# The cosine as one Sin with its turns on ScalarE and VectorE, and a new order for the feed-forward's list

## The chip, the cores and the metric

The kernel runs on one core of one Trainium2 chip. The metric is the device time of one execution in microseconds (us), taken as the median of three runs. Engines are named as in the profile: PE is TensorE's matmuls and PEld its weight loads, DVE is VectorE, ACT is ScalarE, POOL is GpSimd, and SP is SyncE, whose queue issues all DMAs of the feed-forward.

## The reference, cut to what is computed

An attention with a window of 32 tokens and 32 global tokens (4 batches, 8 heads, 512 + 32 tokens, 64 wide) gives x of 2176 tokens by 512. Two feed-forward layers of width 2048 follow:

```python
def _moe_ref(x, w_in, w_out):
    h = x @ w_in
    sp = np.where(h > 20.0, h, np.log1p(np.exp(np.minimum(h, 20.0))))
    g = h * np.tanh(sp)
    return (g @ w_out).astype(np.float32)

def _moe2_ref(x, w_in, w_out):
    h = x @ w_in
    g = h * np.cos(h)
    return (g @ w_out).astype(np.float32)
```

The weight matrices arrive as 64-bit floats, 512 by 2048 and 2048 by 512 for each layer, so the kernel itself has to make 32-bit values of them.

## The kernel before

The attention comes first, by a list of its own (`ORDER`), which the change leaves alone. Beside the attention the first weights are converted and the first products of layer 0 are made. After it, `feed_forward` runs the string `ORDER2`: a list, written out in full, of some 2,700 short steps such as `M0:25` or `h0:24d`. Each step issues one or a few instructions on one engine, in the order of the list; an engine executes its own instructions strictly in that order, and semaphores make it wait for what other engines or DMAs must have done. A letter at the end of a step picks the engine where there is a choice: `a` is ScalarE, `d` VectorE. Where a step stands in the list relative to the steps of another engine binds nothing by itself.

**The work of PE.** The tokens form duos of 768, 768 and 640 columns, the hidden width of a layer 8 pairs of 256. A step number s (0 to 41) is one duo and one pair: steps 0 to 17 are layer 0 (duos of 768, 768 and 640 with six pairs each; the other pairs of layer 0 are worked off ahead, in steps `u` and `lp`), 18 to 41 layer 1 with eight pairs a duo. The pairs of the second duo are taken in reverse. Every value is split into a high and a low part, and a product is the sum of three matmuls. `M0` to `M6` (`product`, L928) are the seven products that give the two halves of the hidden block, by a scheme with sums of blocks that saves one product in eight; each is 6 matmuls of 384 or 320 columns. They go through two PSUM banks: M0, M2, M3 and M4 through bank 0, M1, M5 and M6 through bank 1. `r0`, `r1`, `r2` (`keep`) copy bank 0 out after M0, M2 and M3, and `H00`, `H01`, `H11`, `H10` (`plus` and a copy) give the four quarters of the hidden block after M1, M4, M5 and M6. The next product into the same bank waits for that copy. `U0` to `U11` (`unit`, L1007 in layer 0 and L1011 in layer 1) multiply the activated block by the output weights into six more banks: 8 units a step in layer 0, 12 or 10 in layer 1. The units of step s run among the products of step s+1.

**The activation.** In layer 0 `A` and `B` are Mish on ACT. In layer 1 `gates` makes h cos h for each half c of a step: `k` adds a large constant to h/2pi on ACT (`nearest`, L957), `K` takes it away again on ACT, in a few steps on DVE (`nearest2`, L963, L961), `t` is h/2pi less that on DVE (`turns`, L966), `i` is Sin of pi times it on ACT (L969), `j` its square times 2 on ACT (L972), `p` is (1 - that) times h on DVE (`times`, L975). `h` then splits off the high part on ACT or DVE (L289, L287), and `l` makes the low part on DVE (L809). All work in place on the tile `ks`, one of 768 columns for each half. The last step, 41, does this in quarters of 320 columns.

**The weights.** A piece n (0 to 91) is a quarter or so of a pair's weights. Layer 0's pairs 2 to 7 are pieces 8 to 43, layer 1's pairs 8 to 15 are 44 to 91, six to a pair; piece 89 is the sum block that product M2 of pair 15 reads. `cc` loads the raw words (three buffers `raw`), `cr` is the rounding word (ACT or DVE), `cp` and `cq` the sign (ACT or DVE), `cb` a shift, `cs` the join, `ct` the sign's product, `cx0` to `cx3` the sums of blocks (all DVE), `ch` the high part (ACT or DVE), `cl` the low part (DVE), and `cw` writes the finished piece to DRAM (`scr`). Pieces 8 to 43 are made in the very tiles from which PE reads them. Pieces 44 to 91 go through two staging tiles `co`, taken in turns: `ch` of piece n waits until the DMA of `cw` of piece n-2 has landed. `W0` to `W5` (`fetch`, L914) bring a pair's weights back from `scr` into the tiles `weights` and `even`: W0 for M0 and M1, W1 for M3 and M6, W2 for M4 and M5, W3 for M2, W4 and W5 for the units. A fetch waits on SP's queue for the landing of the `cw` whose bytes it reads and for the last product that read its tile; whatever stands behind it on that queue waits too. Layer 1's first duo (steps 18 to 25) takes the pairs 8 to 15 for the first time, the other duos fetch them again.

Of the kernel before, what the change touches and what calls it, by code (L numbers as in the profile page):

```python
# [75 lines left out]
    u:22 cx3:9 v:9a cb:12 ch:10a st:4 cs:12 u:23 cc:15 v:10a ct:12 cr:14a v:11d pa:0 cl:10 st:5 pa:1 lp:2 pl:0 ch:9a
    cw:10 pl:1 cp:14a cl:9 cq:14a lp:3 T3:0 cw:9 pw:2 cb:13 cs:13 u:24 cc:18 pw:3 ct:13 I4:0a u:25 I3:0d cr:15a L4:0
    u:26 cp:15a L3:0 cq:15a u:27 pa:2 pa:3 lp:4 pl:2 pl:3 lp:5 pw:4 ch:11d cl:11 cw:11 u:28 pw:5 u:29 v:12a u:30 v:13a
    st:6 u:31 v:14a v:15d pa:4 pa:5 lp:6 pl:4 st:7 pl:5 lp:7 pw:6 u:32 pw:7 I5:0d I6:0a L5:0 u:33 T0:1 u:34 u:35 L6:0
    u:36 T1:1 pa:6 pa:7 u:37 pl:6 v:16a pl:7 u:38 v:17a st:8 u:39 v:18a M0:0 v:19a st:9 M1:0 r0:0a u:40 H00:0 u:41 u:42  # L80
# [1028 lines left out]
```

## Time and profile before

| | |
|---|---|
| median of 3 runs | 857.52 us (856.78 to 858.04) |
| profiled execution, its own time | 855.49 us |
| span of its trace | 853.6 us |
| busy share of the span, PE / PEld / DVE / ACT / POOL | 98% / 89% / 75% / 69% / 10% |
| mean granted clock of TensorE, share of full speed | 0.998 |

The span runs from the first to the last instruction; the execution's own time is 1.89 us longer. The feed-forward's products of step 0 start at 213.0 us into the span, the last matmul starts at 849.3 us. A busy share is the union of an engine's instructions over the span. Durations of single matmuls overlap, so the pace of PE is read from the distance between groups.

### The profile page before, as it was taken

The numbers are of one execution on the slowest core, as the hardware profiler recorded it, in microseconds if no ns is written. First come the engines' busy times: TensorE is split into PE (matmuls) and PEld (weight loads), VectorE is DVE, ScalarE is ACT, GpSimd is POOL, SyncE is SP. The second block draws the span as 40 slices with busy tenths as digits, with TensorE's granted clock in tenths as the row PEclk, the third lists the DMA queues.
The fourth block names the chain that finished last, engine by engine and source line by source line (L and its number), as shares of the span: only waits on it lengthen the run. The fifth ranks groups of instructions, "written<-read, shape, count | busy, mean of one in ns | idle before, by whom it ended". The sixth has DMA issues, their size and how long they took to land.

```text
span 853.6 us, 16057 instructions
## 1 busy us (share of the span) xinstructions
PE 839.9 (98%) x5883; PEld 761.0 (89%) x5883; DVE 638.1 (75%) x1336; ACT 590.7 (69%) x1151; POOL 82.1 (10%) x138
## 2 busy tenths in 40 slices
PE   8999999999999999999999999998999999999998
PEld 6788888999999989999999989887889989899996
DVE  6887675794699988759876999999766556865654
ACT  6998888784689967456554587887665455765565
POOL 4664555000000000000000000000000000000000
PEclk9999999999999999999999999999999999999999
DMA  8976852342799899997899889988466556376741
GB/s 179 213 155 163 202 133 64 112 174 83 234 344 319 295 318 350 386 317 237 318 378 354 309 305 337 327 311 292 139 213 198 179 184 184 100 243 224 224 145 66
DMA packets 141565, 198.69 MB, mean 233 GB/s; under 512 B 78896, under 2 KB 98352, under 8 KB 141488
## 3 DMA queue, kind: packets, MB, share of 16 engines
q1 hardware_dynamic: 141488, 197.67, 72.1%
q8 instruction: 47, 0.77, 0.4%
q14 instruction: 30, 0.25, 0.1%
HBM read 148.36 MB, written 49.28 MB: 232 GB/s over the span
## 4 chain that ended last, share of the span: by engine, by line
PE 90%; DMA 3%; ACT 3%; DVE 2%; issue 1%; POOL 0%; SPq 0%; DVEq 0%; POOLq 0%; ACTq 0%
PE bank L928 32%; PE acc L1011 20%; PE acc L1007 15%; PE acc L835 5%; PE h L452 4%; PE s L585 2%; DMA scr<-co 2%; PE av L656 2%; PE bank L452 2%; PE ta L629 2%; PE av L650 1%; PE avg L733 1%; DMA raw<-in_moe_w_in_dram 1%; PE qt L547 1%; PE sg L673 1%; PE kt L561 1%
## 5 line engine op out<-in xcount | busy, mean ns | idle before, releaser
L1011 PE MATMUL acc<-weights,g 128*128 128x512 f32 x816 | 202.7, 394 | 0.3 <-DVE g L809 0.2
L1011 PEld LDWEIGHTS acc<-weights,g 128*128 128x128 f32 x816 | 152.1, 189 | 28.4 <-DVE g L809 0.5
L1007 PE MATMUL acc<-g,weights 128*128 128x512 f32 (+1 forms) x864 | 154.0, 327 | 0.0
L1007 PEld LDWEIGHTS acc<-g,weights 128*128 128x128 f32 x864 | 134.1, 188 | 9.9
L289 ACT COPY r<-bank 128x384 f32<-128x384 f32 (+1 forms) x96 | 44.4, 463 | 113.9 <-PE bank L928 113.5
L943 DVE TENSOR_TENSOR hs<-r,bank 128x384 f32<-128x384 f32 (+1 forms) x126 | 66.8, 530 | 68.7 <-PE bank L928 60.0
L928 PE MATMUL bank<-xo,weights 128*128 128x384 f32 (+1 forms) x504 | 92.7, 328 | 3.9 <-DMA weights<-scr 3.8
L928 PEld LDWEIGHTS bank<-xo,weights 128*128 128x128 f32 x504 | 83.5, 189 | 6.4 <-ACT ks L972 4.1
L966 DVE SCALAR_TENSOR_TENSOR ks<-hs,ks 128x768 f32<-128x768 f32 (+2 forms) x50 | 44.0, 880 | 36.9 <-ACT ks L963 36.7
L605 ACT ACTIVATE pr<-pr,nm 128x160 f32<-128x160 f32 x128 | 53.6, 425 | 6.1 <-DVE nm L602 5.6
L969 ACT ACTIVATE ks<-ks 128x768 f32<-128x768 f32 (+2 forms) x50 | 39.3, 786 | 18.3 <-DVE ks L966 18.2
L289 ACT COPY hs<-bank 128x384 f32<-128x384 f32 (+1 forms) x41 | 18.9, 461 | 47.0 <-PE bank L928 46.9
L835 PE MATMUL acc<-g,weights 128*128 128x384 f32 (+1 forms) x288 | 48.9, 326 | 0.3 <-DVE xT L780 0.3
L928 PE MATMUL bank<-xs,weights 128*128 128x384 f32 (+1 forms) x252 | 48.4, 326 | 0.7 <-ACT r L289 0.7
L928 PE MATMUL bank<-xl,weights 128*128 128x384 f32 (+1 forms) x252 | 48.7, 328 | 0.0
L928 PE MATMUL bank<-xl,even 128*128 128x384 f32 (+1 forms) x252 | 48.6, 328 | 0.0
L928 PE MATMUL bank<-xs,even 128*128 128x384 f32 (+1 forms) x252 | 48.3, 326 | 0.0
L835 PEld LDWEIGHTS acc<-g,weights 128*128 128x128 f32 x288 | 47.6, 188 | 0.4 <-DVE xT L780 0.4
L402 DVE CUSTOM_DVE_ANT_0 bits<-bits,round 128x1024 uint16<-128x1024 uint16 x64 | 45.6, 713 | 1.3
L975 DVE SCALAR_TENSOR_TENSOR ks<-ks,hs 128x768 f32<-128x768 f32 (+2 forms) x50 | 43.9, 878 | 3.5 <-ACT ks L972 2.6
L384 ACT ACTIVATE round<-raw,magic 128x512 f32<-128x512 uint32 x49 | 37.1, 760 | 13.5 <-DVE bits L402 6.7
L809 DVE TENSOR_TENSOR g<-ks,g 128x768 fp32r<-128x768 f32 (+2 forms) x50 | 44.2, 883 | 2.8 <-ACT g L289 1.3
(175 smaller groups left out, 1618.8 us busy)
## 6 DMA issues: line engine op xcount, KB each, us to landing
weights<-scr SPq DMA_DIRECT2D x112, 512.0 KB, 4.7
even<-scr SPq DMA_DIRECT2D x48, 512.0 KB, 4.8
scr<-co SPq DMA_DIRECT2D x40, 512.0 KB, 5.8
raw<-in_moe_w_out_dram SPq DMA_DIRECT2D x28, 512.0 KB, 6.6
raw<-in_moe_w_in_dram SPq DMA_DIRECT2D x26, 512.0 KB, 6.4
scr<-weights SPq DMA_DIRECT2D x21, 512.0 KB, 5.3
weights<-scr SPq DMA_DIRECT2D x32, 256.0 KB, 5.1
scr<-even SPq DMA_DIRECT2D x9, 512.0 KB, 4.4
```

The lines of the kernel that those rows point to most:

```text
L289: nc.scalar.copy(out=out, in_=in_)
L402: nc.vector.tensor_tensor(out=bits(n), in0=bits(n), in1=tiles["round"][:, piece[n] % 2].bitcast(I32), op=ALU.add)
L452: nc.tensor.matmul(t[:, 0:m], l[:, k], r, start=k == 0 and i == 0, stop=k == NK - 1 and i == 2)
L605: nc.scalar.activation(out=pr[:, i], in_=pr[:, i], func=AF.Exp, bias=nm[:, i:i + 1], scale=-1.0, accum_out=l[:, i:i + 1])
L809: nc.vector.tensor_tensor(out=out, in0=x, in1=y, op=ALU.subtract)
L835: nc.tensor.matmul(o, l[:, a * P:(a + 1) * P], r[:, c], start=g == 0 and c == 0 and k == 0, stop=g == 1 and c == 1 and k == 2)
L928: nc.tensor.matmul(to, w[:, l, i + c], x[r][:, c], start=o in (0, 1, 5) and c == 0 and m == 0, stop=c == 1 and m == 2, skip_group_check=True)
L943: nc.vector.tensor_tensor(out=h_of(s, c, i), in0=tiles["r"][:, r, 0:n], in1=tiles["bank"][1][:, 0:n], op=ALU.add)
L966: nc.vector.scalar_tensor_tensor(out=k(s), in0=h(s), scalar=INV2PI, in1=k(s), op0=ALU.mult, op1=ALU.subtract)
L975: nc.vector.scalar_tensor_tensor(out=k(s), in0=k(s), scalar=1.0, in1=h(s), op0=ALU.subtract, op1=ALU.mult, reverse0=True)
L1007: nc.tensor.matmul(o, l[:, cols], r[:, part], start=start and m == 0 and i * a % 2 == 0, stop=stop and m == 2, skip_group_check=True)
L1011: nc.tensor.matmul(tiles["acc"][a], l[:, cols], r, start=start and m == 0, stop=stop and m == 2)
```

## The change

The cosine is computed another way. `k` (`shift`) now makes h/2pi + 0.25 on ACT; `K` (`nearest`) adds and subtracts the large constant in one instruction on DVE and writes the nearest whole number to a new tile `wide`; `t` subtracts it from `ks` on DVE; `i` is one Sin of 2 pi times that on ACT; `j` is gone; `p` is a plain product with h on DVE. The functions can put some of these on GpSimd by a letter `g`, which the new list doesn't contain.

The list `ORDER2` is new from end to end. It holds the same steps but for the 50 `j`. What moved, counted over the list: K in 48 places from ACT to DVE (all 50 are now on DVE); 12 of the steps cp, cq and cr, 17 of r0, r1 and r2 together, 7 of h, 4 of I (the high parts of the inputs) and 2 of ch from DVE to ACT; smaller exchanges elsewhere. The order of PE's products and units is changed inside each step, with the same instructions in number and shape: in layer 0 from `M0 M1 U0 U1 U2 M2 U3 U4 U5 M3 M5 M4 U6 M6 U7` to `M0 U0 M1 U1 M2 U2 U3 M5 M3 U4 M4 U5 M6 U6 U7`, in layer 1 as the two stretches of step 36 in the diff show. The pieces' steps stand earlier or later: the `cw` of piece 89, say, stands after `M0:24` where it stood before `M6:24`.

The diff, cut to its core (the stretches of the list that are shown are around `M0:1`, `M0:6`, `M0:24` and `M0:36`):

```diff
...
-    r2:0a ct:14 cr:18a M4:0 cb:15 ch:14a H11:0 cc:20 u:46 cs:15 cp:18a cl:14 H01:0a M6:0 A0:0 ct:15 cw:14 u:47 H10:0
-    B0:0 cx0:15 y1:0 M0:1 v:22a cx2:15 l0:0 v:23a M1:1 A1:0 st:11 cx1:15 U0:0 cb:18 ch:17a cx3:15 r0:1a cc:21 cl:17 U1:0
...
-    M1:6 ct:43 r0:6a T3:1 I5:1a U0:5 W0:8 H00:6 ch:43a U1:5 L5:1 B1:5 U2:5 cl:43 I4:1a l1:5 cw:43 cc:44 I6:1a M2:6 L4:1
-    U3:5 r1:6a W3:8 L3:1 U4:5 L6:1 U5:5 e0:0 M3:6 T0:2 cc:45 f0:0 cr:44a M5:6 e1:0 y3:0 r2:6a f1:0 cp:44a T1:2 M4:6 y0:1
...
-    U11:22 k1:23 cs:87 M0:24 p0:23 K1:23a M1:24 ct:87 r0:24a W0:25 h0:23a cx0:87 M2:24 W0:27 t1:23 cq:90a W3:27 l0:23
-    W5:24 r1:24a i1:23 cx1:87 U0:23 H00:24 j1:23 U1:23 cx2:87 ch:87d M3:24 cp:91a cl:87 cq:91a p1:23 U2:23 cw:87 r2:24a
-    M5:24 cr:91a cx3:87 h1:23d ch:88a M4:24 l1:23 U3:23 H11:24 H01:24a W2:27 cl:88 U4:23 k0:24 cs:90 W1:25 U5:23 cw:88
-    ch:89a K0:24d U6:23 cl:89 U7:23 t0:24 cw:89 M6:24 ct:90 i0:24 U8:23 cb:91 W1:27 j0:24 H10:24 U9:23 T0:4 U10:23 k1:24
-    U11:23 p0:24 K1:24a W2:25 M0:25 h0:24d W3:25 ch:90a l0:24 M1:25 r0:25a I0:4a t1:24 I1:4a H00:25 cl:90 i1:24 L0:4
-    cw:90 j1:24 M2:25 T1:4 U0:24 r1:25a p1:24 U1:24 T2:4 M3:25 h1:24a W4:25 cs:91 I2:4a U2:24 l1:24 M5:25 r2:25a I3:4a
...
-    h0:35d M0:36 l0:35 W5:36 M1:36 t1:35 r0:36a M2:36 H00:36 W0:38 i1:35 U0:35 j1:35 r1:36d W3:38 U1:35 p1:35 M3:36
-    h1:35d M5:36 l1:35 r2:36a M4:36 H11:36 U2:35 H01:36a W2:38 U3:35 k0:36 U4:35 K0:36a U5:35 W4:37 t0:36 U6:35 M6:36
-    i0:36 U7:35 j0:36 H10:36 W1:38 U8:35 k1:36 p0:36 U9:35 K1:36a h0:36d M0:37 l0:36 W5:37 M1:37 t1:36 r0:37a M2:37
...
+    ct:15 B0:0 u:46 H10:0 ch:14a u:47 l0:0d v:22a v:21a cl:14d v:23a st:10 cx0:15d M0:1 cw:14 A1:0 st:11 cx2:15d cx3:15d
+    ch:17a U0:0 cx1:15d r0:1a cl:17d ch:16a cb:18 M1:1 cw:17 cs:18d ch:15a y1:0 U1:0 B1:0 cl:16d H00:1 cw:16 cp:18a M2:1
...
+    cl:37d U6:3 ch:38a cb:39 W1:7 cw:37 H10:4 B0:4 U7:3 cl:38d cr:39a l0:4d cw:38 M0:5 cq:39a cc:44 cs:39d A1:4 U0:4
...
+    U1:5 W0:8 I4:1a H00:6 M2:6 cp:44a cl:43d cr:44a U2:5 T3:1d cw:43 W3:8 r1:6a L4:1d U3:5 cq:44a I6:1a cb:44 M5:6
...
+    cq:90a cl:86d r2:23a ct:87 U2:22 cw:86 cr:91a H11:23 U3:22 cp:91a cx0:87d M4:23 cx1:87d cq:91a ch:87d cl:87d M6:23
+    H01:23a cx2:87d k0:23 cw:87 U4:22 cx3:87d W0:25 H10:23 ch:88a U5:22 K0:23d k1:23 U6:22 W4:24 t0:23d U7:22 K1:23d
+    i0:23 U8:22 t1:23d U9:22 W1:25 ch:89a p0:23d U10:22 i1:23 U11:22 cl:89d h0:23a cl:88d M0:24 cw:89 W5:24 l0:23d cw:88
+    M1:24 r0:24a p1:23d M2:24 W0:27 H00:24 h1:23a cb:90 U0:23 W3:25 W3:27 r1:24a cs:90d U1:23 l1:23d M3:24 ct:90 M5:24
+    r2:24a cb:91 W2:25 cs:91d ch:90a U2:23 H11:24 U3:23 cl:90d M4:24 ct:91 cw:90 M6:24 T0:4d ch:91a W2:27 H01:24a cl:91d
+    U4:23 W1:27 k0:24 H10:24 U5:23 cw:91 T1:4d k1:24 U6:23 U7:23 K0:24d W4:25 t0:24d U8:23 U9:23 K1:24d i0:24 U10:23
+    t1:24d U11:23 p0:24d i1:24 M0:25 h0:24d M1:25 l0:24d W5:25 r0:25a I0:4a M2:25 p1:24d I1:4a H00:25 U0:24 r1:25a L0:4d
...
+    M0:36 W5:36 p1:35d M1:36 r0:36a h1:35d M2:36 W0:38 H00:36 l1:35d U0:35 r1:36a W3:38 U1:35 M3:36 M5:36 r2:36a U2:35
+    H11:36 M4:36 M6:36 H01:36a W2:38 k0:36 U3:35 H10:36 W1:38 U4:35 K0:36d k1:36 t0:36d U5:35 W4:37 K1:36d U6:35 i0:36
+    t1:36d U7:35 p0:36d U8:35 i1:36 U9:35 h0:36d l0:36d M0:37 W5:37 p1:36d M1:37 r0:37a h1:36d M2:37 W0:39 H00:37 l1:36d
...
-        nc.gpsimd.memset(magic[:, 0:1], MAGIC)
-        nc.gpsimd.memset(magic[:, 1:2], -MAGIC)
-        nc.gpsimd.memset(magic[:, 2:3], 2.0)
+        nc.gpsimd.memset(magic[:, 0:1], 0.25)
+        nc.gpsimd.memset(magic[:, 1:2], 2.0)
...
+    def on():
+        return nc.gpsimd if engine["at"] == "g" else nc.vector
...
+    def minus(out, x, y):
+        on().tensor_tensor(out=out, in0=x, in1=y, op=ALU.subtract)
...
-        nc.vector.tensor_tensor(out=bits(n), in0=bits(n), in1=tiles["round"][:, piece[n] % 2].bitcast(I32), op=ALU.add)
+        on().tensor_tensor(out=bits(n), in0=bits(n), in1=tiles["round"][:, piece[n] % 2].bitcast(I32), op=ALU.add)
...
+        w = lambda s: at(tiles["wide"], s)
         g = lambda s, a: at(g_of(2 * s + c)[a], s)
 
+        def shift(s):
+            nc.scalar.activation(out=k(s), in_=h(s), func=AF.Identity, scale=INV2PI, bias=magic[:, 0:1])
+
         def nearest(s):
-            nc.scalar.activation(out=k(s), in_=h(s), func=AF.Identity, scale=INV2PI, bias=magic[:, 0:1])
-
-        def nearest2(s):
-            if engine["at"] == "d":
-                nc.vector.tensor_scalar(out=k(s), in0=k(s), scalar1=-MAGIC, scalar2=None, op0=ALU.add)
-            else:
-                nc.scalar.activation(out=k(s), in_=k(s), func=AF.Identity, bias=magic[:, 1:2])
+            on().tensor_scalar(out=w(s), in0=k(s), scalar1=MAGIC, scalar2=-MAGIC, op0=ALU.add, op1=ALU.add)
 
         def turns(s):
-            nc.vector.scalar_tensor_tensor(out=k(s), in0=h(s), scalar=INV2PI, in1=k(s), op0=ALU.mult, op1=ALU.subtract)
+            minus(k(s), k(s), w(s))
 
         def sine(s):
-            nc.scalar.activation(out=k(s), in_=k(s), func=AF.Sin, scale=math.pi)
-
-        def square(s):
-            nc.scalar.activation(out=k(s), in_=k(s), func=AF.Square, scale=math.sqrt(2.0))
+            nc.scalar.activation(out=k(s), in_=k(s), func=AF.Sin, scale=2.0 * math.pi)
 
         def times(s):
-            nc.vector.scalar_tensor_tensor(out=k(s), in0=k(s), scalar=1.0, in1=h(s), op0=ALU.subtract, op1=ALU.mult, reverse0=True)
+            on().tensor_tensor(out=k(s), in0=k(s), in1=h(s), op=ALU.mult)
 
         def split(s):
             move(g(s, 0), k(s))
...
-        return {f"k{name}": nearest, f"K{name}": nearest2, f"t{name}": turns, f"i{name}": sine, f"j{name}": square,
+        return {f"k{name}": shift, f"K{name}": nearest, f"t{name}": turns, f"i{name}": sine,
...
+        tiles["wide"] = late.tile([P, 768], F32, name="wide")
```

## Rows read from the trace of the kernel before

**Rows 1.** The page of the kernel before, its first part: busy time of each engine.
```profile
PE 839.9 (98%) x5883; PEld 761.0 (89%) x5883; DVE 638.1 (75%) x1336; ACT 590.7 (69%) x1151; POOL 82.1 (10%) x138
```

**Rows 2.** The chain that ended last: start, length (us), what; over two stretches.
```profile
299.84 3.12 PE bank L928 x18
...
332.04 3.17 PE bank L928 x18
...
378.90 3.12 PE bank L928 x18
...
543.39 3.14 PE bank L928 x18
...
551.77 3.44 PE acc L1011 x15
...
587.07 5.37 DMA scr<-co
592.52 4.15 DMA weights<-scr
...
612.14 3.15 PE bank L928 x18
...
627.79 3.14 PE bank L928 x18
```

**Rows 3.** Stretches (us): busy time and count by engine, granted clock, DMA share, GB/s.
```profile
581.00:596.60 15.60, 11.96 (x60) 10.41 (x58) 13.99 (x23) 11.12 (x17) 0.00 (x0) 1.00 0.91 312
...
643.50:659.20 15.70, 15.70 (x80) 14.16 (x79) 8.96 (x13) 8.41 (x11) 0.00 (x0) 1.00 0.63 186
```

**Rows 4.** PE's waits by releaser: us in total, times, longest.
```profile
PE bank L928 <- DMA weights<-scr: 3.8, 1, 3.8
...
PE bank L928 <- ACT r L289: 0.7, 1, 0.7
...
PE acc L1011 <- DVE g L809: 0.2, 1, 0.2
```

**Rows 5.** Stretches of 1 us behind the long wait, columns as in rows 3.
```profile
597.00:598.00 1.00, 1.00 (x5) 1.00 (x5) 1.00 (x3) 0.00 (x0) 0.00 (x0) 0.61 0.10 29
598.00:599.00 1.00, 1.00 (x5) 0.91 (x4) 0.65 (x2) 0.26 (x1) 0.00 (x0) 0.50 0.19 29
...
600.00:601.00 1.00, 1.00 (x4) 0.77 (x4) 1.00 (x2) 0.68 (x1) 0.00 (x0) 0.68 0.58 217
```

**Rows 6.** ACT's waits by releaser: us in total, times, longest.
```profile
ACT round L384 <- DMA raw<-in_moe_w_in_dram: 5.0, 2, 4.2
```

**Rows 7.** Line 427 (`spill`, the steps `cw`): time from issue to landing.
```profile
DMA to landing us min/median/max: 2.0/5.5/8.8
```

**Rows 8.** Line 914 (`fetch`, the steps `W`): time from issue to landing.
```profile
DMA to landing us min/median/max: 2.7/4.8/8.4
```

**Rows 9.** Groups by line and shape: busy us, mean ns | idle before, releasers.
```profile
L943 DVE TENSOR_TENSOR hs<-r,bank 128x384 f32<-128x384 f32 x84 | 46.4, 552 | 41.1 <-PE bank L928 38.3 <-ACT xo L289 0.8 <-ACT g L289 0.5
...
L289 ACT COPY r<-bank 128x384 f32<-128x384 f32 x68 | 32.5, 478 | 66.5 <-PE bank L928 66.0
...
L809 DVE TENSOR_TENSOR g<-ks,g 128x768 fp32r<-128x768 f32 x32 | 30.6, 958 | 2.3 <-ACT g L289 1.3
L966 DVE SCALAR_TENSOR_TENSOR ks<-hs,ks 128x768 f32<-128x768 f32 x32 | 30.5, 954 | 18.7 <-ACT ks L963 18.5
...
L963 ACT ACTIVATE ks<-ks,magic 128x768 f32<-128x768 f32 x31 | 29.1, 939 | 1.0
...
L969 ACT ACTIVATE ks<-ks 128x768 f32<-128x768 f32 x32 | 27.1, 847 | 11.5 <-DVE ks L966 11.5
...
L422 DVE TENSOR_TENSOR co<-bits,co 128x512 fp32r<-128x512 f32 x24 | 16.5, 688 | 4.5 <-ACT co L289 4.3
...
L289 ACT CAST co<-bits 128x512 fp32r<-128x512 f32 x18 | 11.1, 618 | 2.1 <-DVE bits L414 1.2 <-DMA scr<-co 0.8
```

**Rows 10.** Line 961 (`nearest2` on DVE): durations in ns, min/median/max, and forms.
```profile
L961 DVE TENSOR_SCALAR ks<-ks x2: 320/440/560, 585.1 to 837.4; 128x768 f32<-128x768 f32 x1, 128x320 f32<-128x320 f32 x1
```

More of the change, by code (lines that the diff above doesn't have):

```diff
@@ L76 @@
[L76 to L80, printed above, removed]
@@ new lines @@
+    cl:15d cq:18a cc:21 l1:0d U2:0 cw:15 cr:19a y2:0 r1:1a ct:18 U3:0 cp:19a cb:19 ch:18a cs:19d M5:1 cc:24 cp:20a
+    cl:18d M3:1 cr:20a cb:20 cw:18 cq:20d cq:19a cc:25 U4:0 cs:20d r2:1a ct:20 cr:21a M4:1 H11:1 ch:20a U5:0 ct:19
+    H01:1a cl:20d A0:1 M6:1 ch:19d cw:20 B0:1 cl:19d U6:0 cp:21a cb:21 cw:19 l0:1d cq:21a U7:0 cc:26 cr:24a cs:21d M0:2
+    cp:24a ct:21 cq:24a U0:1 H10:1 r0:2a cx0:21d M1:2 A1:1 cx2:21d cx3:21d ch:23a cx1:21d U1:1 ch:22a H00:2 cl:23d
+    ch:21a cl:22d M2:2 cw:23 B1:1 cl:21d cw:22 U2:1 cr:25a l1:1d cw:21 r1:2a U3:1 cb:24 cp:25a cs:24d cc:27 cq:25a M5:2
@@ L253 @@
     dram = ctx.enter_context(tc.tile_pool(name="dram", bufs=1, space=bass.MemoryType.DRAM))
-    magic = const.tile([P, 3], F32, name="magic")
+    magic = const.tile([P, 2], F32, name="magic")
     weights = wp.tile([P, 8192], F32R, name="weights")
@@ L383, in rounding @@
         else:
-            nc.scalar.activation(out=r, in_=low, func=AF.Identity, scale=2.0 ** -51, bias=magic[:, 2:3])
+            nc.scalar.activation(out=r, in_=low, func=AF.Identity, scale=2.0 ** -51, bias=magic[:, 1:2])
     def sign_of(n):
@@ L413, in run @@
             o, x, y = ((v[0], t[0], v[0]), (t[0], t[1], t[0]), (v[2], t[1], v[0]), (v[1], v[1], v[2]))[i]
-            nc.vector.tensor_tensor(out=o, in0=x, in1=y, op=ALU.subtract)
+            minus(o, x, y)
         return run
@@ L421, in low @@
         hi, lo = halves(n)
-        nc.vector.tensor_tensor(out=lo, in0=value(n), in1=flat(hi), op=ALU.subtract)
+        minus(lo, value(n), flat(hi))
     def spill(n):
@@ L806, in mish @@
         nc.scalar.activation(out=out, in_=in_, func=AF.Mish)
-    def minus(out, x, y):
-        nc.vector.tensor_tensor(out=out, in0=x, in1=y, op=ALU.subtract)
     def late_part(j):
@@ L893, in run @@
             if i == 0:
-                nc.vector.tensor_tensor(out=x_sum(d), in0=a(1, 0), in1=a(1, 1), op=ALU.add)
+                on().tensor_tensor(out=x_sum(d), in0=a(1, 0), in1=a(1, 1), op=ALU.add)
             else:
@@ L1049, in feed_forward @@
             engine["at"] = n[-1:]
-            steps[name](int(n.rstrip("ad")))
+            steps[name](int(n.rstrip("adg")))
     with tc.manual_schedule():
```

256 lines of the change are left out of this document (128 added, 128 removed).

## The prediction

> **What bounds the kernel now.** I read the page's busy shares first, then the chain that ended last, then PE's waits, and then stretches of one step each. PE is busy for 98% of the span [rows 1], and the chain runs over PE's products and units nearly from end to end [rows 2]. A busy share alone would not settle it, so look at the pace: the same group of 18 product matmuls comes back after 15.65 us (612.14 and 627.79), and after 46.86 us over three steps of layer 0 (332.04 to 378.90), that is 15.62 a step [rows 2]. In the stretch from 643.5 us PE is busy for all 15.70 us while DVE works 8.96 and ACT 8.41 [rows 3]. There a faster or slower cosine is worth nothing.
>
> So the question is only where PE falls off this pace, and there are two places that count.
>
> The larger one: from 543.39 to 612.14 us the group comes back after 68.75 us where four steps are 62.60: 6.15 us lost [rows 2]. PE's waits name 3.8 us of it, a product waiting for `weights<-scr` [rows 4]. The chain shows what was late: a write of a staged piece takes 5.37 us from 587.07, its fetch 4.15 us from 592.52, and PE goes on at 596.80 [rows 2]. It is piece 89 (`cw:89`, `W3:25`, product `M2:25`). The list says why. A product is 6 of those matmuls, 3.14/18 x 6 = 1.05 us, a unit 3.44/15 x 3 = 0.69 us [rows 2]. Between `cw:89` and `M2:25` stand three products and four units, 5.9 us; write and fetch need 9.5. That makes 3.6 us, and 3.8 were waited. The wait also drops the clock: the granted clock is 0.61, 0.50 and 0.68 in single microseconds after it [rows 5], and with another 0.50 between them the four from 597 to 601 lose 0.39 + 0.50 + 0.50 + 0.32 = 1.7 us. 0.50 is the 1.2 GHz level. The remaining 0.6 us are small pieces in the three steps before.
>
> The smaller one: 299.84 to 332.04 us is 32.20 where two steps are 31.24: 1.0 us [rows 2], of which PE waited 0.7 for ACT's copy `r1` [rows 4]. ACT stood behind the rounding word of a piece whose raw load had not come, 4.2 us at the longest [rows 6]: `cr:44`, five products and units behind `cc:44`.
>
> **The change, part by part.**
>
> *The order of the pieces.* In the new list `cw:89` stands after `M0:24`. Until `M2:25` come eight products and twelve units, 8 x 1.05 + 12 x 0.69 = 16.7 us, for the same 9.5 us: 7 us to spare. With the longest landings seen, 8.8 us for a write [rows 7] and 8.4 for a fetch [rows 8], it would be 0.5 us late. Going through all `cw` of layer 1 in the same way, this is the shortest lead that is left; the next is 20 us (piece 88). What is late next is therefore not a fetch. `cc:44` moves ahead by a whole step and more: 20 us before its first use instead of 5. I take both losses as gone: -6.15 and -1.0.
>
> *What the earlier conversions run into.* `ch` of a piece waits for the landing of the piece two before it. In the full steps the shortest distances are now `cw:77` to `ch:79`, `cw:86` to `ch:88` (3.5 us each) and `cw:87` to `ch:89` (4.1 us); only the last stands close before a copy that PE needs. A write lands after 5.5 us in the median, between 2.0 and 8.8 [rows 7]. So ACT stands at `ch:89a`, and behind it in its queue are `i1:23`, `h0:23a` and `r0:24a`, for which PE's `M2:24` waits. Counted from `cw:87`: 5.5 landing, 0.62 for `ch` (618 ns), 0.85 Sin (847), about as much for `h0`, 0.48 for `r0` (478) [rows 9] = 8.3 us. `M2:24` is due after eight units and two products, 5.5 + 2.1 = 7.6. That is 0.7 us late. With a landing of 2.0 it is nothing, with 8.8 it is 4.0. I take the median: +0.7.
>
> The Trainium skill, DMA: Bandwidth & Descriptors, section Anatomy of one DMA, fits a transfer as 2.0 us plus its bytes at 436 GB/s, for DMAs that GpSimd issues; these are SP's. By it 512 KB would land after an estimated 3.2 us, `ch:89` would not wait, and the sum would be 0.7 us better. But by the same formula piece 89's write and fetch (256 KB each) take 5.2 us, less than the 5.9 they had, and no wait would have arisen; the trace has 3.8 us, so the measured landings decide.
>
> *The pieces made in place (layer 0).* These are finished just before PE reads them, as before. One is tighter: `ch:14a` stands one unit of step u, about 1 us, ahead of `M0:1`, which needs the low part too. High and low part are 0.62 + 0.69 [rows 9]: 0.3 us late. If the low part of the activations `l0:0d`, ahead of it on DVE, is still running, add up to 0.96 (L809). I take +0.3; below it can be 0.
>
> *The cosine.* Per half of 768 columns ACT loses K (939 ns) and j (as long as the Sin, 847 ns), DVE gains K: 0.56 us by the one such row [rows 9, 10], which subtracts one constant; were the second operation a second pass, 1.1. The products and differences on DVE cost the same as before: L966 has 954 ns, a plain difference (L809) 958 [rows 9]. So a step of layer 1 has some 3.6 us less on ACT and 1.1 us more on DVE, which hides under PE: 10.1 of 15.7 at most in the steps as of [rows 3]. If that cover were gone, the 1.1 us would count in each of 16 steps. In steps 18 to 25 the cover is thin, DVE has 13.99 of 15.60 us there at its busiest place [rows 3]: 16 K add 9.0 us over the eight steps. Against it, 19 instead of 23 pieces are finished in them (4 x some 2.1 us for join, sign and low part, estimated from L422's 688 ns as the length of each), and of the copies that go to ACT several lie here. The load stays near 14 a step, and I put it at 0. The chain from the last quarter of a half to its first unit becomes 0.38 + 0.85 us shorter, which nothing waits for: PE recorded no wait on the activations beyond 0.2 us [rows 4].
>
> *PE's order.* The instructions are the same. In layer 1, M6 now follows M4 at once and needs `H11`, 0.55 us [rows 9], which can begin when M5 ends; U2, U3 and M4 (2.4 us) lie between, in the last duo one unit and one shorter product. It fits where DVE is free: 0. The end of the kernel is the same list: units without a gap to the last matmul, then the copies and stores. GpSimd gets nothing, as no step carries `g`.
>
> Sum: -6.15 - 1.0 + 0.7 + 0.3 = -6.15. The profiled execution took 855.49 us, 1.9 more than its span, which I leave; the median of the runs is 2.0 above it. From the median, 857.52 - 6.15 = **851.4 us**. Three runs of the kernel lie within 0.15%, and I count 0.2%, 1.7 us, as what a measurement can tell.
>
> **The rivals.**
>
> *Part is given back* (0.18). The waits at the staging tiles or a late piece in steps 1 to 5 cost more than I take: one landing of 8.8 us adds 3.3, five steps each 0.3 later add 1.5. If PE then waits long enough to lose its clock, another 1.7. For it: ACT and DVE wait at the `co` tiles already [rows 9], and by the list steps 1 to 7 are as full as before. Against: of those waits in the old list only the ones in piece 89's chain reached PE. 853 to 856 us.
>
> *The stall only moves* (0.07). SP's queue is strict, and `W3:25`, `W3:27` and `W2:25` now wait on it for the writes of pieces 89 and 88 while `cw:90` and `cw:91` stand behind. If one fetch comes 4 us late there, the 6 us are lost again: 857. Against: leads of 16 us and more.
>
> *DVE becomes the bound: slower* (0.05). `H11` of each of the 24 steps of layer 1 now has some 2.4 us where it had twice that; in the last duo about 1.6. If K and t in front of it make DVE late by more than about 1.1 us beyond that place, each further tenth costs 2.4 us over 24 steps. From 0.33 us on, 7.9 us, the change is slower by over 0.2%; at 0.45 it is 862. Against: in [rows 3] DVE idles for over 6 us of a step.
>
> *PE has room of its own* (0.02). PE's weight loads are busy 14.16 of 15.70 us in a full step [rows 3], so the new mixture of products and units could run at a better pace, 0.1 us a step over 42 steps: 847. Against: the same groups keep one pace in every full step. The Trainium skill, Perfetto Trace Analysis, section Identifying the Most-Contended Engine, holds weight-load busy time a better measure of what TensorE has left than matmul busy time; by that rule 11% would be left, and the constant pace of the rows speaks for the matmuls.
>
> *The change doesn't do what it says* (0.01): counted in the list, it does.
>
> **How the numbers follow.** The likeliest case (0.67) has 849.4 to 853: below, the two added costs vanish and the small pieces of layer 0 and step 19 go as well; above, the added costs double. The range 848.8 to 855.2 takes in most of the first rival and leaves out the others. Faster by over 0.2% (below 855.8): 0.67, 0.02 and nearly all of 0.18, so 0.86. Within 0.2%: 0.09. Slower: 0.05.
>
> **What would show it.** Right: no wait of PE on `weights<-scr`, the group of 18 matmuls at 15.65 us throughout steps 19 to 27, a granted clock of 1.00 there, no 0.7 us in step 6; a wait of some tenths at `M2:24` and `M0:1`; ACT's busy time down by some 50 us and DVE's about the same. Wrong: a wait of PE on an ACT copy or a DVE quarter that recurs step by step, or one over 2 us on a piece with the clock falling behind it.

## The result: 847.6 us, about one per cent faster, and 1.2 us below the range

The changed kernel takes 847.57 us in the median (847.00 to 848.08, 4 runs); the ratio to the kernel before is 0.9892 (95% interval 0.9871 to 0.9913). In a second set of runs it took 847.53 us, ratio 0.9905 (0.9890 to 0.9920). The forecast was 851.4 us, range 848.8 to 855.2: faster, as forecast, but by more. The kernel before is the one that scatters: its median is 857.5 in the three runs that were shown, and between 854.9 and 855.5 in four later sets of 11 to 23 runs each. Below, therefore, ratios to the kernel before in the same set are compared, and in the traces the starts of PE's instructions.

**The profile after.** The page's first part, which answers [rows 1], and the head of PE's waits by releaser (us in total, times, longest), which answers [rows 4]:

```profile
PE 835.1 (99%) x5883; PEld 757.6 (90%) x5883; DVE 640.6 (76%) x1339; ACT 539.9 (64%) x1098; POOL 82.5 (10%) x137
```

```profile
PE heat L749 <- POOL ident masks.py:199: 1.4, 1, 1.4
PE s L591 <- ACT sg L695: 1.1, 1, 1.1
PE bank L931 <- ACT r L292: 0.6, 2, 0.4
```

The wait for `weights<-scr` is gone; the first two lines lie in the attention. ACT has 50.8 us less to do, DVE 2.5 more. The chain of work in layer 1 (start, length, what) answers the later half of [rows 2]:

```profile
604.44 3.14 PE bank L931 x18
...
620.01 3.14 PE bank L931 x18
...
635.59 3.15 PE bank L931 x18
```

The group of 18 comes back after 15.57 and 15.58 us, where it was 15.65. Three stretches of one step each (busy us and count of PE, PEld, DVE, ACT, POOL, then granted clock, DMA share, GB/s) answer [rows 3]; the first two are the steps that lost their stall:

```profile
573.13:588.71 15.58, 15.58 (x80) 14.07 (x78) 14.50 (x22) 7.47 (x12) 0.00 (x0) 1.00 0.96 324
588.71:604.28 15.57, 15.57 (x79) 14.07 (x78) 14.64 (x21) 10.58 (x16) 0.00 (x0) 1.00 0.34 128
635.43:651.00 15.57, 15.57 (x80) 14.07 (x78) 9.29 (x14) 5.50 (x8) 0.00 (x0) 1.00 0.71 249
```

PE is busy throughout and the clock is at 1.00. All of the span, from the starts of the first matmuls (`M0` of a step, `u:0`) in two profiled executions of each kernel, in us:

| stretch | before | again | after | again |
|---|---|---|---|---|
| span's start to `u:0` (attention) | 157.15 | 156.14 | 156.16 | 155.97 |
| `u:0` to `M0:0` | 55.87 | 55.86 | 55.35 | 55.38 |
| steps 0 to 17 (layer 0) | 268.19 | 267.97 | 268.49 | 268.19 |
| of these, step 6 | 16.60 | 16.41 | 15.60 | 15.60 |
| of these, steps 1, 4 and 8 | 46.88 | 46.88 | 48.18 | 47.67 |
| steps 18 to 23 | 93.33 | 93.30 | 93.13 | 93.17 |
| steps 24 and 25 | 37.44 | 37.12 | 31.15 | 31.14 |
| steps 26 to 33 | 125.17 | 125.18 | 124.59 | 124.59 |
| step 34 to the last matmul | 112.12 | 112.12 | 112.15 | 112.15 |

The first row is no effect: the list of the attention is the same, and the kernel before does it in 156.14 us too. The other rows make 7.3 us between the first profiles and 6.9 between the second. So steps 24 and 25 carry most of the gain, as forecast. Against the gain stands a cost that the table doesn't show: each execution of the changed kernel takes 2.2 to 2.3 us more than its span, each of the kernel before 1.8 to 1.9. All kernels below with the new functions have the former, all with the old ones the latter, so the new cosine costs 0.4 us outside the span; what this time is stays open. The experiments ask which part of the change gives the gain.

### The profile page after: what moved, and what is told of

Its sections match the earlier page's. It is cut to its first block, busy times and chain, and to the rows that moved or that the text cites. A ratio compares the mean times of both kernels' runs of the same rounds, so it can differ in the third digit from the quotient of the medians.

```text
span 845.1 us, 16028 instructions
## 1 busy us (share of the span) xinstructions
PE 835.1 (99%) x5883; PEld 757.6 (90%) x5883; DVE 640.6 (76%) x1339; ACT 539.9 (64%) x1098; POOL 82.5 (10%) x137
## 4 chain that ended last, share of the span: by engine, by line
PE 89%; DMA 4%; ACT 3%; DVE 3%; issue 1%; SPq 0%; POOL 0%; DVEq 0%; ACTq 0%
PE bank L931 31%; PE acc L1009 22%; PE acc L1005 13%; PE acc L838 6%; PE h L458 4%; PE s L591 2%; PE av L662 2%; PE bank L458 2%; DMA scr<-co 2%; PE ta L635 2%; PE av L656 1%; PE avg L739 1%; DMA raw<-in_moe_w_in_dram 1%; DMA stage<-part 1%; PE sg L679 1%
## 5 line engine op out<-in xcount | busy, mean ns | idle before, releaser
L1009 PE MATMUL acc<-weights,g 128*128 128x512 f32 x816 | 198.6, 391 | 0.0
L1005 PE MATMUL acc<-g,weights 128*128 128x512 f32 (+1 forms) x864 | 159.5, 327 | 0.0
L292 ACT COPY r<-bank 128x384 f32<-128x384 f32 (+1 forms) x113 | 52.3, 463 | 124.1 <-PE bank L931 123.1
L961 ACT ACTIVATE ks<-hs,magic 128x768 f32<-128x768 f32 (+2 forms) x50 | 43.9, 879 | 6.4 <-DVE hs L946 4.8
L931 PE MATMUL bank<-xo,even 128*128 128x384 f32 (+1 forms) x252 | 46.6, 327 | 0.3 <-DVE hs L946 0.3
L390 ACT ACTIVATE round<-raw,magic 128x512 f32<-128x512 uint32 x52 | 39.4, 760 | 10.1 <-DVE bits L408 6.3
L301 DVE TENSOR_TENSOR ks<-ks,wide 128x768 f32<-128x768 f32 (+2 forms) x50 | 44.2, 883 | 1.6
```

What stands on the lines that cost most here:

```text
L292: nc.scalar.copy(out=out, in_=in_)
L301: on().tensor_tensor(out=out, in0=x, in1=y, op=ALU.subtract)
L390: nc.scalar.activation(out=r, in_=low, func=AF.Identity, scale=2.0 ** -51, bias=magic[:, 1:2])
L931: nc.tensor.matmul(to, w[:, l, i + c], x[r][:, c], start=o in (0, 1, 5) and c == 0 and m == 0, stop=c == 1 and m == 2, skip_group_check=True)
L961: nc.scalar.activation(out=k(s), in_=h(s), func=AF.Identity, scale=INV2PI, bias=magic[:, 0:1])
L1005: nc.tensor.matmul(o, l[:, cols], r[:, part], start=start and m == 0 and i * a % 2 == 0, stop=stop and m == 2, skip_group_check=True)
```

## The experiments

Each kernel was timed in turns with the kernel before on the same chip; *before_again* and *m6_late* were executed once, for their profile.

### The two halves of the change, each alone

*list_alone*: the new list, the old functions, a `j` behind each `i` and `K` on ACT throughout.

```diff
-    U7:28 K1:29d i0:29 U8:28 t1:29d U9:28 p0:29d i1:29 U10:28
+    U7:28 K1:29a i0:29 j0:29 U8:28 t1:29d U9:28 p0:29d i1:29 j1:29 U10:28
```

> The new list of the feed-forward with the old cosine: behind each Sin stands its Square on ScalarE again, and both passes of the rounding are on ScalarE. My theory: the time comes from the list (the stall at piece 89, the wait in step 6), and the cosine lies beside PE. Then this kernel takes what the changed one takes, 847.5 us, at most 1 us more, and a full step of layer 1 lasts 15.57 us as after the change, because the order of PE's products and units sets it. The rival, the cosine carries part of the gain: 850 us or more, with the step at 15.65.

*cosine_alone*: the old list without `j` and with every `K` on DVE, the new functions.

```diff
-    U8:27 H10:28 W1:30 j0:28 U9:27 k1:28 p0:28 U10:27 U11:27 K1:28a h0:28d
+    U8:27 H10:28 W1:30 U9:27 k1:28 p0:28 U10:27 U11:27 K1:28d h0:28d
```

> The old list with the new cosine, the Squares dropped and the second rounding pass on VectorE throughout. My theory: 857 us within 1 us, the product of piece 89 still waits some 4 us for its fetch in step 25, and a full step of layer 1 lasts 15.65 us. The rival, that ScalarE with some 50 us less work finishes piece 89 earlier: part of the 6.15 us of step 25 is gone, 852 to 855. The rival that the cosine sets the pace: steps of 15.57 us, about 1 us less over layer 1.

| | old cosine | new cosine |
|---|---|---|
| old list | 1 | 1.0017 (1.0007 to 1.0027) |
| new list | 1.0092 (1.0075 to 1.0109) | 0.9905 (0.9890 to 0.9920) |

My theory fell. The list alone is slower than the kernel before, 863.0 us, and the cosine alone is no gain either, 856.34 us. Only together are they faster. (The `j` were put directly behind the `i`; other places for them in the new list were not tried.) What holds list_alone is in PE's waits, from 480 us on:

```profile
PE bank L930 <- ACT r L291: 10.8, 9, 3.0
```

All are products `M2` that wait for the copy `r0`. ACT's timeline in step 19 (start, length, what, [idle before <- releaser]) shows why; first list_alone, then the changed kernel:

```profile
493.79 0.85 ACT L971 ACTIVATE ks<-ks 128x768 f32<-128x768 f32 x1
494.67 0.85 ACT L974 ACTIVATE ks<-ks 128x768 f32<-128x768 f32 x1
495.43 0.60 ACT L291 CAST co<-kept 128x512 fp32r<-128x512 f32 x1
495.93 0.93 ACT L965 ACTIVATE ks<-ks,magic 128x768 f32<-128x768 f32 x1
496.77 0.81 ACT L291 CAST g<-ks 128x768 fp32r<-128x768 f32 x1
497.49 0.47 ACT L291 COPY r<-bank 128x384 f32<-128x384 f32 x1
```

```profile
493.85 0.85 ACT L970 ACTIVATE ks<-ks 128x768 f32<-128x768 f32 x1
494.60 0.61 ACT L292 CAST co<-kept 128x512 fp32r<-128x512 f32 x1
495.73 0.84 ACT L292 CAST g<-ks 128x768 fp32r<-128x768 f32 x1 [0.52 <-DVE ks L973]
496.47 0.47 ACT L292 COPY r<-bank 128x384 f32<-128x384 f32 x1
```

L974 is the Square and L965 the second pass of the rounding; with them ACT has no gap ahead of the copy, and `r0` starts a microsecond later although the Sin began at the same time. PE then waits for 1.95 us, and behind the wait the granted clock falls. The stretches of step 19, columns as above, list_alone first:

```profile
493.81:513.15 19.34, 17.39 (x80) 15.26 (x79) 11.83 (x18) 13.76 (x21) 0.00 (x0) 0.91 0.73 270
```

```profile
494.35:510.57 16.22, 15.82 (x80) 14.00 (x79) 14.76 (x24) 10.50 (x17) 0.00 (x0) 1.00 0.87 320
```

ACT is busy for 13.76 of 19.34 us: not full, but in a row ahead of a copy that is due. In cosine_alone it is the other engine, in the same step:

```profile
494.62:511.23 16.61, 16.18 (x81) 14.02 (x79) 16.29 (x29) 9.15 (x14) 0.00 (x0) 1.00 0.85 308
```

DVE has 16.29 of 16.61 us, as the old list keeps conversions on DVE that the new one gives to ACT; steps 19, 21, 24 and 25 are 0.2 to 1.4 us longer than before, and the stall of step 25 stays, at 22.71 us. The pace, on the other hand, is the list's: undisturbed steps of list_alone last 15.57 us (28 to 32), those of cosine_alone 15.65.

### How much of ScalarE's time the new list needs

*list_and_squares*: as list_alone, but `K` stays on DVE, so only the Squares are added. *rounding_on_scalar*: the changed kernel with `K` on ACT, no Squares; its pass adds a constant and doesn't round, so the Sin gets other arguments.

```diff
-            on().tensor_scalar(out=w(s), in0=k(s), scalar1=MAGIC, scalar2=-MAGIC, op0=ALU.add, op1=ALU.add)
+            nc.scalar.activation(out=w(s), in_=k(s), func=AF.Identity, bias=magic[:, 0:1])
```

> The new list with the old cosine once more, but the second pass of the rounding is on VectorE, as in the new cosine, so ScalarE has only the Squares in addition (847 ns each, two in a step of layer 1). Theory: the new list needs the time that the new cosine leaves on ScalarE; list_alone lost 15.4 us against the changed kernel because Square and second pass (0.85 + 0.94 us a half) stand ahead of the copies r0 to r2. With half of that extra the loss is between, 2 to 9 us over the changed kernel: 850 to 857 us. The rival, that only the second pass on ScalarE does the harm: within 1 us of the changed kernel. The rival, that the Squares alone do it: 860 or more.

> The changed kernel with the rounding pass on ScalarE: one pass of the same size that adds a constant instead of rounding, 0.94 us, with no Squares. Theory: any extra pass of this length on ScalarE in front of the copies r0 costs about what the Squares cost (0.85 us each, 3.4 us in all), whichever it is: 850 to 852.5 us, the loss in the same steps (19, 21, 23, 27) at M2. The rival, that the longer chain from the products to the units does it, so that a pass that moves from VectorE to ScalarE costs only 0.4 us a half: within 1 us of the changed kernel.

Measured: 850.89 us, ratio 0.9946 (0.9930 to 0.9962), and 851.15 us, ratio 0.9957 (0.9945 to 0.9969), against 847.53 us and 0.9905 for the changed kernel, both as expected. By the medians the Squares cost 3.4 us, the second pass 3.6, both together 15.5; by the ratios, as these sets ran on different chips, 3.5, 4.4 and 16.0. Either way both together cost about twice the sum. Both kernels lose at `M2` of steps 19, 21 and 23, and of one or two more each. A row of the changed kernel's ACT tells why one pass is nearly borne and two are not, `r0` in step 24:

```profile
574.40 0.48 ACT L292 COPY r<-bank 128x384 f32<-128x384 f32 x1 [1.13 <-PE bank L931]
```

ACT stood ready 1.13 us before PE. One pass of 0.85 or 0.94 us fits into that, two of 1.79 don't. That this slack is the reason in each step was worked out from this row, not tried.

*rounding_twice*: the changed kernel with every `K` issued twice.

```diff
-    K0:28d k1:28 t0:28d
+    K0:28d K0:28d k1:28 t0:28d
```

> The changed kernel with the rounding pass on VectorE issued twice (the same result twice): 0.55 us more per half, 1.1 us a step, 26 us of VectorE over layer 1. Theory: VectorE's work lies under PE's. In the steps from 26 on, where VectorE has 10.9 to 11.8 of 15.6 us, nothing changes; in steps 18 to 24, where it has 13 to 15, PE may wait some tenths a step; 847.5 to 850 us. The rival, that VectorE's copies behind the products are due at once (the chance I gave for the slower outcome): each of 24 steps is later by the 1.1 us or much of it, over 857.

Measured: 852.39 us, ratio 0.9966 (0.9954 to 0.9978): 4.9 us (5.2 by the ratios) for 24 us more of DVE's work (664.7 against 640.6 us), above my 850, far below 857. Steps 28 to 32 stay at 15.57; steps 19, 22, 23, 26, 27, 34 and 41 lose 0.3 to 1.0 us each. PE doesn't wait there for DVE's copies behind the products, as my rival had it, but again for ACT's `r`, and once, for 0.9 us ahead of the first unit of step 40, for a low part from DVE. Its waits from 480 us on, and ACT ahead of `r0` in step 26:

```profile
PE bank L932 <- ACT r L293: 2.3, 4, 0.9
```

```profile
607.47 0.84 ACT L293 CAST g<-ks 128x768 fp32r<-128x768 f32 x1 [1.96 <-DVE ks L974]
608.39 0.84 ACT L293 CAST xl<-xT 128x768 fp32r<-128x768 f32 x1
609.13 0.47 ACT L293 COPY r<-bank 128x384 f32<-128x384 f32 x1
```

ACT stands for 1.96 us until DVE has finished the product `p` (L974), and the copy stands behind it. DVE is busy for 15.5 of the 15.8 us of the step before. So DVE's work, too, reaches PE by way of ACT's queue.

### What the stall of step 25 consisted of

*before_again* is the kernel before, unchanged.

> The kernel before unchanged, for a second profile of it. If the waits at piece 89 and the first 10 us are the same from one execution to the next, step 25 lasts 21.29 us and the heads' part starts its feed-forward at 157.15 us again, and the 1.7 us between the profiled execution and the median lie elsewhere. The rival, that the wait on the transfers differs from execution to execution: step 25 lasts 20 to 24 us.

853.92 us in the profiled execution, with the wait and step 25 nearly the same (3.5 and 20.98 us). So that stall does not make the scatter; the attention took 1.0 us less. In the nine traces with the old list `u:0` starts between 156.1 and 158.1 us and layer 0 takes 267.3 to 269.8; in the eight with the new list it is 155.9 to 157.3 and 267.9 to 268.5. Why these differ from execution to execution was not followed up.

*no_wait_89* and *no_wait_88_89* read the weights of step 25 from an older pair, so no late write is waited for.

```diff
-    scratch[p, 0]
+    scratch[p - (s == 25 and i == 3), 0]      # no_wait_89:    W3:25
+    scratch[p - (s == 25 and i > 1), 0]       # no_wait_88_89: W2:25 and W3:25
```

> The kernel before with one fetch changed: the quarter of the weights for step 25 that holds piece 89 is fetched from the same quarter of the pair of step 24, written long before, so that nothing waits for piece 89; the product of step 25 computes with those weights. All else, lists and cosine, is that of before. My theory: the 6.15 us of steps 24 and 25 are gone but for the small pieces ahead of them, 857.2 - 5.5 to 6.2 = 851 to 851.7 us, and the clock stays at 1.00 there. The rival, that the stall only moves (PE is held by something else a little later, or ScalarE is late in the steps after): 854 or more. If the time falls below 850.5, the stall costs more in most executions than in the profiled one, and the gain of the change that I did not forecast lies there.

> As no_wait_89, and the fetch that stands ahead of it in SyncE's queue, with piece 88, comes from the pair of step 24 as well; the product of step 25 computes with those weights. Theory: no_wait_89 gained nothing because its fetch stood in the queue behind this one, which waited for the write of piece 88. Without both waits the 3.8 us of PE's wait and the half clock behind it are gone: step 25 lasts 15.65 to 16.2 us in place of 21.2, the whole 5 to 5.6 us less than before, ratio 0.9935 to 0.9945. The rival, that the stall only moves (the fetches themselves are late, or another piece): step 25 still above 18 us, ratio over 0.996.

Neither gained, against both expectations: ratios 0.9999 (0.9989 to 1.0009) and 0.9993 (0.9980 to 1.0006), step 25 at 21.24 and 20.72 us. The chain of no_wait_88_89:

```profile
588.90 1.08 PE bank L928 x6
...
590.00 0.32 SPq L914
590.32 0.05 issue
590.37 0.91 SPq L914
...
591.33 6.78 DMA weights<-scr
```

The six matmuls are `M6:24`. Behind them SP may issue `W1:27`, which overwrites what they read, and only behind that, on the same queue, `W2:25` and `W3:25`. From 591.33 the fetch itself takes 6.78 us. So the late place on the queue holds `M2:25` as long as the late write does.

*fetch_early* takes away both: the two fetches read a pair written long before (two pairs back) and stand behind `M2:24`.

```diff
-    cx0:87 M2:24 W0:27 ...  p0:24 K1:24a W2:25 M0:25 h0:24d W3:25 ch:90a
+    cx0:87 M2:24 W3:25 W2:25 W0:27 ...  p0:24 K1:24a M0:25 h0:24d ch:90a
```

> The kernel before with both fetches of no_wait_88_89 (now from the pair of step 23, written earlier still; the product of step 25 computes with those weights) and with their places in the list moved: both stand behind the product M2 of step 24, where the new list has the one of piece 89. Theory: no_wait_88_89 gained nothing because in the old list the two fetches stand in SyncE's queue behind a fetch that may go only when PE has done M6 of step 24, some six us before M2 of step 25, and a fetch there lands after 4 to 7 us; the late piece and the late place each hold the product for the same time. With both taken away step 25 lasts 15.65 to 16.2 us in place of 21, 5 to 5.6 us in all, ratio 0.9935 to 0.9945. The rival, that the stall moves to another transfer: step 25 above 18 us and the ratio over 0.996.

Ratio 0.9954 (0.9940 to 0.9967), step 25 at 18.60 us: half of the stall is gone, where I had expected all of it to go. PE no longer waits for a fetch, but at `M2:25`, `M3:25` and `M4:25` for `r0` to `r2`. Part of its chain:

```profile
578.71 7.41 DMA scr<-co
...
586.55 4.95 DMA scr<-co
...
591.52 0.62 ACT co L286
592.14 0.39 ACT r L286
```

`ch:90a` stood on ACT until the write from its staging tile had landed, with `r0:25` behind it. Three kernels separate the rest.

> The kernel before with a third staging tile for the last six pieces (86 to 91), in a part of another tile that is idle in those steps; lists, fetches and cosine are those of before. So the conversion of piece 89 waits for the write of 86, long landed, not for that of 87. Theory: ScalarE stood at the staging tiles; the conversions of 88 to 90 and the writes of 88 and 89 go some 2 us earlier, and step 25 loses 1 to 3 of its 5.3 us; ratio 0.996 to 0.999, since the fetches still stand behind M6 of step 24. The rival, that the staging tiles are no cause: step 25 above 20.8 us.

> fetch_early (both fetches of step 25 from an earlier pair and at an earlier place) and the third staging tile of third_tile together. Theory: the 3 us that step 25 still lost in fetch_early were ScalarE's waits at the staging tiles, 2.6 us at piece 89 and more at piece 90, with r0 to r2 behind them; step 25 lasts 15.65 to 16.3 us, in all 2.4 to 2.9 us less than fetch_early. The rival, that ScalarE is simply too full there (Squares and second passes): step 25 above 17.5 us.

> fetch_early with the new cosine in the old list: no Squares, the rounding on VectorE; the staging tiles are two again. Theory of the staging tiles: ScalarE still waits for the writes of 87 and 88, less work behind these waits; step 25 gets back 0.5 to 1.5 of the 3 us, 17 to 18 us. The rival, that Squares and second passes fill ScalarE: step 25 lasts 15.65 to 16.3 us.

| kernel | step 25, us | ratio |
|---|---|---|
| before (second profile) | 20.98 | 1 |
| third_tile | 21.32 | 1.0000 (0.9989 to 1.0011) |
| fetch_early | 18.60 | 0.9954 (0.9940 to 0.9967) |
| fetch_early_cosine | 18.51 | 0.9978 (0.9968 to 0.9988) |
| fetch_early_third | 16.72 | 0.9940 (0.9924 to 0.9956) |

```diff
-        i = (n - 8) % 2
+        i = (n - 8) % (3 if n >= 86 else 2)
+        if i == 2:
+            return tiles["stage"][:, 0:1024].bitcast(F32R)
```

The third staging tile alone does nothing (I had expected 1 to 3 us), since the fetch is late anyway; behind the early fetch it takes 1.9 us more off step 25 (expected 2.4 to 2.9). The intervals of fetch_early and fetch_early_third overlap, so this rests on step 25 in their traces. The new cosine in its place takes next to nothing (18.51, expected 17 to 18): ACT waited for writes there, not for its own work. Its ratio is the worse because the new cosine costs the old list time elsewhere, in steps 19, 21 and 24 as in cosine_alone. 1.1 us of step 25 are left in fetch_early_third, of which PE waits 0.6 us for a copy `r`. So the stall had three causes side by side: a late write, a late place on the queue, and ACT behind the staging tiles. The late write and the staging tiles were each taken away alone, and neither showed anything, because the next cause holds the same product; the late place alone was not tried.

### The pace of PE

*m6_late*: the changed kernel with the old order in steps 29 to 32, `M6` behind the eighth unit.

> The changed kernel with the order of the old list in four full steps of layer 1 (29 to 32): product 6 stands behind the eighth unit again, not behind product 4. Theory: PE loses some 10 ns at each of the first units behind a product, so one switch more between products and units costs 0.08 us: these four steps last 15.65 us, the others 15.57. The rival, that the pace comes from elsewhere in the list: 15.57 throughout.

849.92 us in its one execution. Its chain:

```profile
652.56 3.14 PE bank L929 x18
...
668.21 3.36 PE bank L929 x18
...
684.07 3.36 PE bank L929 x18
```

Step 29 lasts 15.65 us, as expected. The next three last 15.86, which I did not expect: the group itself is longer, 3.36 in place of 3.14, as `M2` starts 0.11 us late and itself takes 0.11 us longer; which step of my arrangement does that was not followed up. So step 29 alone speaks for the order. Its matmuls show where the 0.08 goes, by the time from the start of each product or unit to the next one's (ns):

```
after    M3=1045 M5=1040 U2=698 U3=691 M4=1044 M6=1040 U4=698 U5=691 U6=692 U7=680 U8=680 U9=680
m6_late  M3=1044 U2=699 M5=1061 M4=1040 U3=699 U4=691 U5=691 U6=680 U7=680 M6=1066 U8=698 U9=691 U10=692
```

Step 29 of the kernel before has the numbers of m6_late, to 1 ns. The first product behind one or more units takes up to 26 ns more than the others, and the first three units behind products 10 to 20 ns more than the later ones. One change to and fro less saves 0.08 us a step. This holds for the full steps of layer 1 only: in layer 0 products and units last 1039 to 1041 ns in either order (an undisturbed step 15.60 before and after), and the steps of the last duo went from 13.02 to 13.01.

### A version with the table's load moved

*mended* is the changed kernel with two steps moved ahead of conversions, and one Sin of a single column in an idle stretch.

```diff
-    U7:2 l0:3d cw:32 ... cr:36a H10:3 cx0:33d
+    U7:2 H10:3 l0:3d cw:32 ... cr:36a cx0:33d
-    ch:50a M3:8 cl:50d U4:7 r2:8a cw:50 H11:8 M4:8
+    M3:8 U4:7 r2:8a ch:50a H11:8 M4:8 cl:50d cw:50
-    M6:18 H01:18a
+    M6:18 warm:18 H01:18a
+        steps["warm"] = lambda s: nc.scalar.activation(out=tiles["wide"][:, 0:1], in_=magic[:, 0:1], func=AF.Sin)
```

> The changed kernel with three of its remaining waits taken up: H10 of step 3 stands ahead of four conversions on VectorE (M1 of step 4 waited 0.4 us for its bank), r2 of step 8 ahead of a conversion on ScalarE that waits for a staging tile (M4 of step 8 waited up to 0.3 us), and one Sin of a single column stands behind M6 of step 18, so that the load of the function table, 1.28 us ahead of the first Sin of layer 1, falls into an idle stretch of ScalarE (M2 of step 19 waited 0.8 us). Theory: step 3 loses 0.4 us, step 8 up to 0.5, step 19 0.6 to 0.9; 1 to 1.8 us in all, 845.7 to 846.5 us. The rival, that the table load only moves and holds the copy H01 of step 18: step 18 or 19 is longer by as much, 847.5 us.

Measured: 846.34 us, ratio 0.9897 (0.9885 to 0.9910). Step 19 lasts 15.55 us in place of 16.22 and 16.53 in the two executions of the changed kernel. There the load of the function table stood directly ahead of the first Sin and the copy `r0`; now it lies ahead of a copy for which ACT had stood idle for 0.99 us:

```profile
487.92 1.28 ACT L1043 ACT_TABLE_LOAD   x1
489.22 0.20 ACT L1043 ACTIVATE wide<-magic 128x1 f32<-128x1 f32 x1
489.33 0.46 ACT L290 COPY hs<-bank 128x384 f32<-128x384 f32 x1
```

The Trainium skill, ScalarE activation tables: per-element evaluation and per-set limits, section What a function is on this engine, puts functions of different sets one load of 1283 ns apart; the trace agrees, 1.28 us. Of the other two edits no gain can be seen: `M1:4` no longer waits, but `M2:4` then waits 0.4 us for its weights, and step 8, now 15.60 us, had lost 0.5 us in one execution of the changed kernel and nothing in the other. The interval overlaps that of the changed kernel, so that this version is the faster one rests on the trace of step 19.

## Why the prediction was right or wrong, point by point

The forecast lies 3.8 us above the measured time. About 2.4 of it are the base from which I subtracted, the rest is the gain, put too small above all by PE's order, which I had at nothing. That the sum of -6.15 comes near the traces is in part luck. Net of the 0.4 us outside the span they give -6.9 and -6.5, but the wait of +0.7 did not come, and losses of +0.5 to +1.0 and 1.3 us saved by PE's order were not forecast.

**The 6.15 us of the stall: right in size, wrong in its account.** Steps 24 and 25 became 6.29 us shorter in the first profiles and 5.98 in the second. But I put all of it on the distance from piece 89's write to `M2:25`. no_wait_88_89 takes the write away and gains nothing, and fetch_early_third shows that the place of the fetch and the staging tiles must go as well. In the new list, which moves all three, PE waits for nothing in these steps.

**Step 6, -1.0: right.** 16.60 to 15.60 us (16.41 to 15.60 in the second profiles).

**The wait at `M2:24`, +0.7: did not come.** In the stretch of that piece, 562 to 572 us, two writes were issued; they landed after 3.2 us in the median and the one of piece 87 after 2.9, not the 5.5 of [rows 7]. ACT's `ch:89a` waited for nothing, and took 0.39 us in place of 0.62, as a sum block has half the columns. The row of the DMA issues there (KB each, median us to landing), and ACT's row:

```profile
scr<-co SPq DMA_DIRECT2D x2, 512.0 KB, 3.2
```

```profile
570.65 0.39 ACT L292 CAST co<-kept 128x256 fp32r<-128x256 f32 x1
```

By the formula of the Trainium skill, DMA: Bandwidth & Descriptors, section Anatomy of one DMA, 512 KB take an estimated 3.2 us, without a wait here; at this place the trace agrees. Over all writes of the changed kernel, of 256 to 512 KB, it doesn't (its landing times, min/median/max):

```profile
DMA to landing us min/median/max: 2.0/5.8/11.1
```

**The pieces made in place, +0.3: right where I named it, but not all.** `M0:1` takes 1.33 us in place of 1.07. With two losses that I did not see, steps 1, 4 and 8 are 1.3 us longer in the first profiles and 0.8 in the second. In step 4 `M1:4` stood behind `H10:3`, which stood behind four conversions on DVE (0.5 us). In step 8, in one of two executions, `M4:8` waited for ACT's `r2`, which stood behind a conversion into a staging tile (0.5 us).

**PE's order, 0: the step that failed.** "The instructions are the same" holds, but not the pace: 15.57 in place of 15.65 us in some ten undisturbed full steps, 0.8 us. I asked only whether `M6` would wait for `H11`, not how long the same matmuls last in another order. I had this as a rival with a chance of 0.02 and argued against it from the constant pace of equal groups, which compares only steps of one order. The way to `M0:0` is 0.5 us shorter as well; list_alone has this with the old cosine, so it is the list's.

**The cosine, 0: failed as reasoned.** I wrote of a full step that there "a faster or slower cosine is worth nothing". For such steps it holds in either list: steps 28 to 32 of list_alone last 15.57 us. It doesn't hold for the new list in most of steps 19 to 27, in 33 to 35 and in the last, where the engines also make pieces or inputs or move results: there ACT's copies come so close behind its other work, to which the list adds some 40 steps from DVE, that the old cosine costs 15.5 us. I counted the 3.6 us a step that ACT gets free, and gave them no worth. The time that the cosine frees pays for the list; without it the list made the kernel slower. The price on DVE was right: `K` with both operations takes 0.55 us in the median, not 1.1 (ns, min/median/max):

```profile
L964 DVE TENSOR_SCALAR wide<-ks x50: 318/553/564, 490.6 to 832.6; 128x768 f32<-128x768 f32 x32, 128x640 f32<-128x640 f32 x14, 128x320 f32<-128x320 f32 x4
```

**The base: the larger part of the miss.** I subtracted from 857.52, the median of three runs that lay within 0.15%, and left aside that the profiled execution took 855.49. Four later sets put the kernel before at 854.9 to 855.5 us; 855.1 - 6.15 is 849.0, 1.4 us above the measured time, and a range moved down with it would have held it. The gain itself was forecast at 6.15 and is 6.8 to 9.4 us by the second ratio, so both the base and the terms were off, by some 2.4 us and by 1 to 2. Why the first runs of the kernel before were slower stays open.

**What would show it.** No wait on `weights<-scr`, a clock of 1.00 and no 0.7 us in step 6 came as said, and so did the wait at `M0:1`; the pace of 15.65 did not stay, and the wait at `M2:24` is missing. Of the rivals, DVE as the bound is not what the change met, but rounding_twice shows how near it is: a second pass costs 4.9 us, by way of ACT's copies and not of `H11`.

## What to carry to other kernels

An edit that is worth nothing where it stands can be what another edit lives on: of two changes that come together, measure all four corners before one is called the cause. When a stall has a named releaser, ask what would hold the same instruction if that one were early; here the queue and the staging tiles stood right behind the write, and the repairs that were tried alone measured zero. And on an engine in strict order look less at its busy share than at what stands ahead of the short copy that PE waits for.
